# A test of the softmax sums at the end of the kernel, and a second path behind a branch

## The chip, the cores and the metric

The kernel runs on one core of a Trainium2 chip. The metric is the device time of one execution in microseconds. The engines of a core are TensorE (PE, matmuls), VectorE (DVE), ScalarE (ACT), GpSimd (POOL) and SyncE (SP). Each has its own queue of instructions and runs it in order; between queues, semaphores say what is done. PEld is PE's loading of weights, and a name with a q (ACTq) is an engine's queue itself, for example when it issues a transfer.

## The reference

The first half is a dynamic convolution: each position has its own softmax weights over its last 7 positions, for each of 8 heads of 24 columns. The second half is a layer with two input matrices, an elementwise maximum and an output matrix.

```
x: (8, 4160, 192) = 0.1 * normal;  weight_gen: (8, 4160, 8 heads, 7 taps) = 0.3 * normal
w = exp(weight_gen - max over taps);  w = w / (sum of w over taps + 1e-9)
y[s] = sum over taps t of w[s, head, t] * x[s - 6 + t]      (zeros ahead of each sequence)
h1 = y @ w1;  h2 = y @ w2                                   (192 -> 1024)
out = maximum(h1, h2) @ w_out                               (1024 -> 192), 33280 rows
```

## The kernel before

The 33,280 rows lie over 128 partitions, 260 neighbouring rows ("columns" in the code, `CPP`) on each. The columns go in 17 batches of 16 (the last has 4). The softmax is computed without the maximum: `exp_sum(b)` takes the exponential of a batch on ScalarE, `red(b)` sums the 7 taps on VectorE (L147), `ln(b)` takes the logarithm of the sum in place on ScalarE (L151), `shift(b)` subtracts it from the raw weights on VectorE (L156), and `weights(b, o)` takes the exponential again on ScalarE, now normalized, in bfloat16 (L167). The sums of a batch live in a tile from a pool with three buffers, `psm`, so they are gone three batches later.

`mul` and `adds` (L182, L198, L202, L205) form and add the seven products on VectorE; a DMA transposes the result (L214), and GpSimd's small `gate` cast (L222) waits for that transposition before GpSimd issues the next loads. On PE, `hid_tile` (L297) makes the hidden layer as differences of the two matrices, `relu` (L307, ScalarE) moves it out of PSUM, and the output comes from two kinds of matmuls, `out_first` (L349 with the product of w1 and w_out, and half of L337) and `out_second` (the other half of L337). Because max(h1, h2) = h1 + relu(h2 - h1), this gives the reference's maximum. `evac` copies results out of PSUM on ScalarE (L393) and has SyncE store them.

The order of each queue is written out by hand (a manual schedule): what stands earlier in the code is earlier in its engine's queue. The end is `rest_of_results` (L484): the last columns in three parts, `out_first` of each ahead of `out_second` of the one before, and `evac` behind it. The last `evac` copies into `o_last` (L381), and ScalarE and SyncE issue one store each (L384). Behind that stands the closing block (line L801 in the profile): SyncE waits for all transfers and engines, every queue drains, and GpSimd gathers and releases all five queues, twice.

Of the kernel before, what the change touches and what calls it, by code (L numbers as in the profile page):

```python
# [9 lines left out]
FP32 = mybir.dt.float32  # L10
BF16 = mybir.dt.bfloat16
I32 = mybir.dt.int32
AF = mybir.ActivationFunctionType
ALU = mybir.AluOpType
AX = mybir.AxisListType


def _sub(base: bass.AP, off: int, dims):
    ap = [list(base.ap[0])] + [[int(s), int(c)] for s, c in dims]
    return dataclasses.replace(base, offset=base.offset + off, ap=ap)  # L20
# [3 lines left out]
def kernel(  # L24
# [9 lines left out]
    nc = tc.nc  # L34

    B, S, D = x.shape
    H, K = weight_gen.shape[2], weight_gen.shape[3]
    F = moe_w1.shape[1]
    P = 128
    PAD = K - 1  # L40
    WGC = H * K
    FCH = F // P
    HF = F // 2
    CPP = B * S // P
    RPB = P // B
    G = D // H
# [3 lines left out]
    BATCHES = [(c, min(16, CPP - c)) for c in range(0, CPP, 16)]  # L50
    NB = len(BATCHES)
# [11 lines left out]
    UNITS = []  # L63
    for b, (c0, n) in enumerate(BATCHES):
# [3 lines left out]
    TILES = [(u, k) for u, (_, _, n) in enumerate(UNITS) for k in range(n)]  # L68
# [6 lines left out]
    consts = ctx.enter_context(tc.tile_pool(name="consts", bufs=1))  # L75
    pwg = ctx.enter_context(tc.tile_pool(name="pwg", bufs=4))
    pxb = ctx.enter_context(tc.tile_pool(name="pxb", bufs=2))
    pe_ = ctx.enter_context(tc.tile_pool(name="pe", bufs=2))
    psm = ctx.enter_context(tc.tile_pool(name="psm", bufs=3))
    pm = ctx.enter_context(tc.tile_pool(name="pm", bufs=1))  # L80
    pen = ctx.enter_context(tc.tile_pool(name="pen", bufs=2))
    py = ctx.enter_context(tc.tile_pool(name="py", bufs=2))
    pyt = ctx.enter_context(tc.tile_pool(name="pyt", bufs=6))
    prd = ctx.enter_context(tc.tile_pool(name="prd", bufs=7))
    first_ps = ctx.enter_context(ExitStack())
    ps = {k: first_ps.enter_context(tc.tile_pool(name="pps_" + k, bufs=2, space=bass.MemoryType.PSUM))
          for k in ("h", "o")}
# [6 lines left out]

    wg_ts, xb_ts, e_ts, s_ts, en_ts, y_ts, yt_ts = {}, {}, {}, {}, {}, {}, {}

    m_t = pm.tile([P, K * 16 * D], BF16, name="m_t")
# [37 lines left out]
    def part(b, i, of):  # L137

        n = BATCHES[b][1]
        h0, h1 = n * i // of * H, n * (i + 1) // of * H  # L140
        return slice(h0, h1), h0 * K, [[K, h1 - h0], [1, K]]

    def red(b, i=0, of=1):
        if i == 0:
            s_ts[b] = psm.tile([P, BATCHES[b][1] * H], FP32, name="sum_t", tag="sum")
        hs, at, ap = part(b, i, of)
        nc.vector.reduce_sum(out=s_ts[b][:, hs], in_=_sub(e_ts[b], at, ap), axis=AX.X)  # L147

    def ln(b, i=0, of=1):
        s_t = s_ts[b][:, part(b, i, of)[0]]  # L150
        ln_of[b] = nc.scalar.activation(out=s_t, in_=s_t, func=AF.Ln)  # L151

    def shift(b, i=0, of=1):
        hs, at, ap = part(b, i, of)
        w_t = _sub(wg_ts[b], at, ap)
        nc.vector.tensor_tensor(out=w_t, in0=w_t, in1=_sub(s_ts[b], hs.start, [[1, hs.stop - hs.start], [0, K]]),  # L156
                                op=ALU.subtract)

    def weights(b, o):
# [73 lines left out]
    def half(j):  # L233
        return slice(64 * j, 64 * j + 64)
# [23 lines left out]
    relu_of, yt_of, w10_of, ln_of = {}, {}, [], {}  # L258
# [6 lines left out]
    rd_at, hd_at, op_at, o_t = {}, {}, {}, []  # L265
# [43 lines left out]

    def column(c):  # L310

        b = min(c // 16, NB - 1)
        for u, (ub, o, n) in enumerate(UNITS):
            if ub == b and o <= c - BATCHES[b][0] < o + n:
                k = c - BATCHES[b][0] - o
                return u, k // 2, k % 2

    def place(p):
# [5 lines left out]
    def op_out(c):  # L324

        tile_, at = op_at[c // 2]
        return tile_[:, at + c % 2 * 512:at + c % 2 * 512 + D]

    def out_hidden(c, f, r):

        u, i, j = column(c)
        t0 = TILES.index((u, 0))
        if UNITS[u][2] == 8:
            (rd, k), at = rd_at[t0 + f], j * 512 + i * P
        else:
            (rd, k), at = rd_at[t0 + f // 2], j * 512 + f % 2 * 256 + i * P
        return nc.tensor.matmul(  # L337
            op_out(c), lhsT=rd[half(r), k * 1024 + at:k * 1024 + at + P],
            rhs=wo[half(r), f * D:(f + 1) * D], start=False, stop=(r != j and f == FCH - 1),
            skip_group_check=True,  # L340
        )

    def out_first(now):

        for c in now[::2]:
            u, i, _ = column(c)
            for s in range(3):
                for j in range(2):
                    nc.tensor.matmul(  # L349
                        op_out(c + j),  # L350
                        lhsT=yt_ts[u][half(j), (3 * i + (s + j) % 3) * P:(3 * i + (s + j) % 3 + 1) * P],
                        rhs=w10[half(j), s * D:(s + 1) * D], start=(c == now[0] and s == 0),
                        stop=False, skip_group_check=True,
                    )
            for f in range(FCH):
                last = [out_hidden(c + j, f, j) for j in range(2)]
        return last

    def out_second(now, go):

        for c in now[::2]:
            for f in range(FCH):
                for j in range(2):
                    mm = out_hidden(c + 1 - j, f, j)
                    if c == now[0] and f == 0:
                        tc.add_manual_dep(mm.ins, go.ins.name, SYNC, reason="bank of the other half")

    def relay(last):

        go = nc.scalar.nop()  # L370
        for mm in last:
            tc.add_manual_dep(go.ins, mm.ins.name, SYNC, reason="bank of the other half")
        return go
# [52 lines left out]
    OUTS, c = [[], [], []], 0  # L426
    for g in range(3, len(GROUPS)):
        most = 4 if g == 3 else 2 if GROUPS[g][1] == 2 or len(OUTS[-1]) == 4 else 4
        n = min(most, ready[g] - c)
# [5 lines left out]
    def room(g):  # L435

        t0, n = GROUPS[g]
        if "c" in ps:
            for t, k in zip(range(t0, t0 + n), "abc"[:n - 1] + "c"):
                hd_at[t] = ps[k].tile([P, 1024], FP32, name="hd" + k, tag=k), 0  # L440
        else:
            for t in range(t0, t0 + n):
                hd_at[t] = ps["h"].tile([P, 1024], FP32, name="hdp", tag="hd"), 0
        rd = prd.tile([P, 3 * 1024], BF16, name="rd_t", tag="rd")
        for t in range(t0, t0 + n):
            rd_at[t] = (rd, t - t0)
        return rd

    def out_room(now, tag=None):
        tag = tag or ("r" if "r" in ps else "o")  # L450
        tile_ = ps[tag].tile([P, 1024], FP32, name="op_ps", tag=tag if tag in "abc" else "op")
        for c in now:
            op_at[c // 2] = tile_, (c - now[0]) // 2 * D

    def hidden(g, now=(), between=lambda: None, beside=lambda: None, ahead=lambda: None,
# [25 lines left out]
        if len(now) <= 2:  # L481
            beside()

    def rest_of_results(c):  # L484

        parts = [p for p in (c[:4], c[4:-2], c[-2:]) if p]
        assert max(map(len, parts)) <= 4
        go = []
        for i, now in enumerate(parts):
            out_room(now, ("r", "a", "c")[i])  # L490
            go.append(relay(out_first(now)))
            if i:
                out_second(parts[i - 1], go[i - 1])
                evac(parts[i - 1][0] // 2, len(parts[i - 1]) // 2)
        out_second(parts[-1], go[-1])
        evac(parts[-1][0] // 2, len(parts[-1]) // 2)
# [6 lines left out]
    ident = consts.tile([P, P], BF16, name="ident")  # L503
    msk_i = consts.tile([P, 1], I32, name="msk_i")
    msk = consts.tile([P, 1], FP32, name="msk")
    gate = consts.tile([P, 1], FP32, name="gate")
    o_last = consts.tile([P, 2 * D], FP32, name="o_last")

    with tc.tile_pool(name="pstage", bufs=1) as pstage:
# [7 lines left out]
        for p0, p1 in ((1, 16), (16, P)):  # L517
            nc.sync.dma_start(
                out=xs[p0:p1, 0:PAD * D],
                in_=bass.AP(tensor=x.tensor, offset=(p0 * CPP - PAD) * D,  # L520
                            ap=[[CPP * D, p1 - p0], [1, PAD * D]]),
# [20 lines left out]
        for wi, wsrc in enumerate((moe_w1, moe_w2)):  # L542
            for h in range(2):
                nc.sync.dma_start(  # L544
                    out=ws["T", wi][half(h), :],
                    in_=bass.AP(tensor=wsrc.tensor, offset=P * F + h * HF, ap=[[F, 64], [1, HF]]),
# [11 lines left out]
        for step in (exp_sum, red, ln, shift):  # L558
            for i in range(2):
# [4 lines left out]
                                op0=ALU.mult)  # L564
        nc.scalar.activation(out=xb_ts[0][:, HP:PAD * D], in_=xs[:, HP:PAD * D], func=AF.Copy,
                             scale=msk[:, 0:1])
        for o in (0, 4, 8, 12):
            weights(0, o)
        nc.vector.tensor_copy(out=xb_ts[0][:, PAD * D:(PAD + 4) * D],
                              in_=xs[:, PAD * D:(PAD + 4) * D])  # L570
# [36 lines left out]
        def keep_warm(times):  # L607
# [11 lines left out]
            out=wo[:, :].rearrange("p (f d) -> p f d", d=D),  # L619
            in_=bass.AP(tensor=moe_w_out.tensor, offset=0, ap=[[D, P], [P * D, FCH], [1, D]]),  # L620
# [9 lines left out]
        rd = room(0)  # L630
# [43 lines left out]
        rd = room(3)  # L674
# [17 lines left out]
        rd = room(4)  # L692
# [2 lines left out]

    pout = ctx.enter_context(tc.tile_pool(name="pout", bufs=1))
    o_t.append(pout.tile([P, 24 * D], FP32, name="o_t", tag="o"))


    def rest_of_1():  # L700
# [64 lines left out]
    for g in range(4, len(GROUPS)):  # L765
# [7 lines left out]
        else:  # L773
            hidden(g, OUTS[g], beside=lambda: steps(g, tiles), before=lambda: softmax_steps(g, 0),
                   after=lambda: softmax_steps(g, 1))
    rest_of_results(OUTS[-1])

# [1 line left out]
_INS = ['x', 'weight_gen', 'moe_w1', 'moe_w2', 'moe_w_out']  # L779
# [26 lines left out]
```

## Time and profile before

| what | value |
|---|---|
| median of 3 timed runs | 408.99 us (406.66 to 411.06) |
| the profiled execution | 406.16 us |
| its span, first to last instruction | 404.3 us |
| outside the span | 1.9 us |
| busy in the span: PE, DVE, ACT, POOL | 98%, 92%, 89%, 19% |
| granted TensorE clock, mean | 0.999 |

A timeline row has the start in the span, the length, the engine, the source line, the operation, what it writes and reads, and how many such instructions it joins. A group's row ends with total busy time and the mean of one in nanoseconds, and then idle time ahead of it with what ended that. In the records of one source line, the three numbers behind an operation are its shortest, median and longest duration in nanoseconds, and then come the first and the last start in microseconds. The digits are the busy tenths of 40 equal slices of 10.1 us. In the list of DMA queues a row has packets, megabytes and the share of the time of 16 DMA engines.

### The profile page before, as it was taken

Reading aid. Unit: us, or ns where it says so; the run is one execution under the profiler, and the core shown is the slowest. Engines: PE = TensorE matmul, PEld = TensorE weight load, DVE = VectorE, ACT = ScalarE, POOL = GpSimd, SP = SyncE. Lnnn points to the kernel's source line nnn. Section 1 sums busy time; section 2 is a strip of 40 time slices with the busy share of each in tenths; the row PEclk is TensorE's granted clock in tenths of the full one; section 3 lists DMA queues with packets and bytes.
Section 4 is the critical chain, followed back from the end, with each engine's and each line's share of the span. In section 5 each row is a group of like instructions: output and inputs, shape, how many; then the busy total and the mean of one; then the engine's idle time right before and its main releaser. Section 6 shows DMA issues by size and latency. Waiting matters only on the chain.

```text
span 404.3 us, 16242 instructions
## 1 busy us (share of the span) xinstructions
PE 397.3 (98%) x7458; PEld 318.6 (79%) x7458; DVE 370.3 (92%) x215; ACT 360.7 (89%) x462; POOL 76.3 (19%) x101
## 2 busy tenths in 40 slices
PE   7999999999999999999999999999999999999996
PEld 2699999777777787778777778877787877777795
DVE  5999999999999999999999999999999999999100
ACT  6899999999999989999899999989999899897872
POOL 0311130212222011222221212222012222110000
PEclk9999999999999999999999999999999999999999
DMA  8956549876757855774775587577548647743614
GB/s 250 232 120 184 157 98 245 149 174 155 194 90 232 191 111 121 229 204 78 233 201 109 115 237 203 74 236 200 110 111 240 170 70 241 154 89 51 246 41 158
DMA packets 60785, 65.70 MB, mean 163 GB/s; under 512 B 47631, under 2 KB 49039, under 8 KB 60718
## 3 DMA queue, kind: packets, MB, share of 16 engines
q1 hardware_dynamic: 52334, 40.54, 35.6%
q0 software_dynamic: 8240, 24.04, 29.2%
q8 instruction: 58, 0.95, 0.9%
q10 hardware_dynamic: 144, 0.10, 0.1%
q14 instruction: 9, 0.07, 0.1%
HBM read 35.96 MB, written 25.56 MB: 152 GB/s over the span
## 4 chain that ended last, share of the span: by engine, by line
PE 92%; ACT 3%; DMA 2%; SPq 1%; issue 0%; DVE 0%; DVEq 0%; ACTq 0%
PE op_ps L337 42%; PE hdc L297 13%; PE hda L297 13%; PE hdb L297 13%; PE op_ps L349 8%; PE yps L246 2%; DMA ws1T<-in_moe_w_dram 2%; ACT rd_t L307 1%; PE hdp L297 1%; SPq L544 0%; ACT yt L253 0%; PE pw L652 0%; ACT w1t L670 0%; ACT e_t L135 0%; SPq L536 0%
## 5 line engine op out<-in xcount | busy, mean ns | idle before, releaser
L337 PE MATMUL op_ps<-wo,rd_t 64*128 64x192 bf16 x4160 | 210.3, 243 | 0.0
L337 PEld LDWEIGHTS <-rd_t 64*128 64x128 bf16 x4160 | 180.6, 94 | 15.5
L182 DVE TENSOR_TENSOR m_t<-xb_t,en_t 128x10752 bf16<-128x10752 bf16 (+1 forms) x37 | 187.4, 5070 | 0.3
L297 PEld LDWEIGHTS <-wd 64*128 64x128 bf16 x1776 | 93.4, 94 | 40.1 <-issue 1.1
L307 ACT ACTIVATE rd_t<-hdc 128x1024 bf16<-128x1024 f32 x82 | 84.0, 1024 | 17.6 <-PE hdc L297 15.9
L222 POOL CAST gate<-yt 128x1 f32<-128x1 bf16 x29 | 41.1, 1416 | 267.3 <-DMA yt<-y_t 267.3
L307 ACT ACTIVATE rd_t<-hdb 128x1024 bf16<-128x1024 f32 x81 | 83.6, 1032 | 0.0
L307 ACT ACTIVATE rd_t<-hda 128x1024 bf16<-128x1024 f32 x81 | 83.4, 1030 | 0.0
L198 DVE TENSOR_TENSOR m_t<-m_t 128x4608 bf16<-128x4608 bf16 (+1 forms) x29 | 72.7, 2508 | 0.1
L297 PE MATMUL hdc<-yt,wd 64*128 64x512 bf16 (+1 forms) x534 | 67.8, 359 | 0.0
L393 ACT COPY o_t<-op_ps 128x384 f32<-128x384 f32 (+1 forms) x99 | 56.3, 579 | 12.6 <-PE op_ps L337 12.6
L297 PE MATMUL hda<-yt,wd 64*128 64x512 bf16 (+1 forms) x528 | 67.0, 359 | 0.0
L297 PE MATMUL hdb<-yt,wd 64*128 64x512 bf16 (+1 forms) x522 | 67.0, 362 | 0.0
L349 PE MATMUL op_ps<-w,yt 64*128 64x192 bf16 x780 | 55.3, 243 | 0.0
L349 PEld LDWEIGHTS <-yt 64*128 64x128 bf16 x780 | 38.8, 94 | 15.6 <-issue 0.5
L202 DVE TENSOR_TENSOR m_t<-m_t 128x3072 bf16<-128x3072 bf16 (+1 forms) x29 | 49.9, 1722 | 0.1
L167 ACT ACTIVATE en_t<-wg_t 128x896 bf16<-128x896 f32 (+2 forms) x45 | 35.2, 809 | 2.0 <-PE op_ps L337 2.0
L205 DVE TENSOR_TENSOR y_t<-m_t 128x1536 bf16<-128x1536 bf16 (+1 forms) x29 | 27.3, 941 | 0.5
L114 POOL DMA_DIRECT2D xb_t<-in_x_dram x33 | 18.0, 546 | 21.3 <-DVE m_t L182 10.4
L156 DVE TENSOR_TENSOR wg_t<-wg_t,sum_t 128x280 f32<-128x280 f32 (+5 forms) x46 | 22.0, 481 | 0.0
L147 DVE TENSOR_REDUCE sum_t<-e_t 128x64 f32<-128x448 f32 (+2 forms) x31 | 19.5, 633 | 2.3 <-ACT e_t L135 2.3
L135 ACT ACTIVATE e_t<-wg_t 128x896 f32<-128x896 f32 (+2 forms) x18 | 15.9, 889 | 2.3 <-DMA wg_t<-in_weight_gen_dram 2.3
(49 smaller groups left out, 117.1 us busy)
## 6 DMA issues: line engine op xcount, KB each, us to landing
out_dram<-o_t SPq DMA_DIRECT2D x27, 768.0 KB, 4.5
xb_t<-in_x_dram POOLq DMA_DIRECT2D x30, 384.0 KB, 4.9
wg_t<-in_weight_gen_dram POOLq DMA_DIRECT2D x14, 448.0 KB, 5.6
xb_t<-xb_t POOLq DMA_DIRECT2D x16, 288.0 KB, 5.1
out_dram<-o_t SPq DMA_DIRECT2D x10, 384.0 KB, 3.1
wg_t<-in_weight_gen_dram SPq DMA_DIRECT2D x2, 448.0 KB, 4.2
xs<-in_x_dram SPq DMA_DIRECT2D x2, 384.0 KB, 6.0
xb_t<-in_x_dram POOLq DMA_DIRECT2D x3, 192.0 KB, 4.6
```

Of the source, the lines that this page charges most:

```text
L156: nc.vector.tensor_tensor(out=w_t, in0=w_t, in1=_sub(s_ts[b], hs.start, [[1, hs.stop - hs.start], [0, K]]), op=ALU.subtract)
L167: nc.scalar.activation(out=_sub(en_ts[b], (o * WGC + j * N * K) * 2, [[2 * N, K], [2, N], [1, 2]]), in_=_sub(wg_ts[b], (o * H + j * N) * K ...
L182: return nc.vector.tensor_tensor(out=m_out, in0=x_in, in1=_sub(en_ts[b], o * WGC * 2, [[2, K * n * H], [0, G // 2], [1, 2]]), op=ALU.mult,)
L198: nc.vector.tensor_tensor(out=taps(0, 1, 3), in0=taps(0, 1, 3), in1=taps(3, 1, 3), op=ALU.add)
L202: nc.vector.tensor_tensor(out=taps(0, 2, 2), in0=taps(0, 2, 2), in1=taps(1, 5, 2), op=ALU.add)
L205: nc.vector.tensor_tensor(out=_sub(y_ts[b], o * D, [[64, 2], [P, 3 * w // 2], [1, 64]]), in0=taps(0, 1, 1), in1=taps(2, 1, 1), op=ALU.add,)
L222: nc.gpsimd.tensor_copy(out=gate, in_=yt[:, 0:1])
L297: nc.tensor.matmul(hid_out(t, f, j), lhsT=wd_at(j, s, f // 4, f % 4 * P, P), rhs=_sub(yt_ts[u][half(j), :], (s + j) % 3 * P, [[3 * P, w // ...
L307: relu_of[t0] = nc.scalar.activation(out=rd[:, k * 1024:(k + n) * 1024], in_=hd[:, at:at + n * 1024], func=AF.Relu)
L337: return nc.tensor.matmul(op_out(c), lhsT=rd[half(r), k * 1024 + at:k * 1024 + at + P], rhs=wo[half(r), f * D:(f + 1) * D], start=False, s ...
L349: nc.tensor.matmul(op_out(c + j), lhsT=yt_ts[u][half(j), (3 * i + (s + j) % 3) * P:(3 * i + (s + j) % 3 + 1) * P], rhs=w10[half(j), s * D: ...
L393: nc.scalar.copy(out=_sub(o, c % 24 * D, [[D, len(qs)], [h * D, 2], [1, D]]), in_=_sub(tile_, at + (qs[0] - p) * D, [[D, len(qs)], [512, 2 ...
```

## The change

The sums of all batches are kept: `red` writes into slices of two tiles that live to the end, `sums` (128 columns) and `sums_later` (the other 132), and `ln` writes its logarithm to a tile of its own, which `shift` reads. In `rest_of_results`, after the first part's `out_first`, a test follows: the largest and the smallest sum of each partition are compared with 1e15 and 1e-15, and a matmul with one column on each side counts the partitions that are good. At the very end four engines (all but SyncE) load that count into a register and branch: where it is not 128, a second path computes all 260 columns again, four at a time and with the maximum subtracted first, written out without a loop, with its transfers on GpSimd.

```
 def red(b, i=0, of=1):
     if i == 0:
-        s_ts[b] = psm.tile([P, BATCHES[b][1] * H], FP32, name="sum_t", tag="sum")
+        c0, n = BATCHES[b]
+        at = c0 - 128 if c0 >= 128 else c0
+        s_ts[b] = sums[c0 >= 128][:, at * H:(at + n) * H]
+        ln_ts[b] = psm.tile([P, n * H], FP32, name="ln_t", tag="ln")
...
 def ln(b, i=0, of=1):
-    s_t = s_ts[b][:, part(b, i, of)[0]]
-    ln_of[b] = nc.scalar.activation(out=s_t, in_=s_t, func=AF.Ln)
+    hs = part(b, i, of)[0]
+    ln_of[b] = nc.scalar.activation(out=ln_ts[b][:, hs], in_=s_ts[b][:, hs], func=AF.Ln)
...
+LOW, HIGH = 1e-15, 1e15
+def test_sums():
+    good, ones = in_range[:, 4:5], in_range[:, 5:6]
+    for i, s in enumerate(sums):
+        nc.vector.tensor_reduce(out=in_range[:, i:i + 1], in_=s, axis=AX.X, op=ALU.max)
+        nc.vector.tensor_reduce(out=in_range[:, 2 + i:3 + i], in_=s, axis=AX.X, op=ALU.min)
+    nc.vector.memset(ones, 1.0)
+    nc.vector.tensor_scalar(out=in_range[:, 0:2], in0=in_range[:, 0:2], scalar1=HIGH, scalar2=None, op0=ALU.is_le)
+    nc.vector.tensor_scalar(out=in_range[:, 2:4], in0=in_range[:, 2:4], scalar1=LOW, scalar2=None, op0=ALU.is_ge)
+    nc.vector.tensor_reduce(out=good, in_=in_range[:, 0:4], axis=AX.X, op=ALU.min)
+    found = ps["b"].tile([P, 1024], FP32, name="found", tag="b")
+    nc.tensor.matmul(found[0:1, 0:1], lhsT=good, rhs=ones, start=True, stop=True)
+    nc.vector.tensor_copy(out=count, in_=found[0:1, 0:1])
...
 def rest_of_results(c):
...
         go.append(relay(out_first(now)))
+        if i == 0:
+            test_sums()
...
+sums = [consts.tile([P, 128 * H], FP32, name="sums")]
+in_range = consts.tile([P, 6], FP32, name="in_range")
+count = consts.tile([1, 1], I32, name="count")
...
+sums.append(pout.tile([P, (CPP - 128) * H], FP32, name="sums_later"))
...
 rest_of_results(OUTS[-1])
+ET = mybir.EngineType
+good = nc.values_load(count, engines=[ET.PE, ET.Activation, ET.DVE, ET.Pool], min_val=0, max_val=P,
+                      skip_runtime_bounds_check_because="a count of partitions")
+with tc.If(good != P, preferred_fallthrough_block=False):
+    with_maximum()
```

`with_maximum()` calls `columns(c)` 65 times, for c = 0, 4, ... 256. Each loads the raw weights and the rows, subtracts the maximum, takes the exponential, the sum and the logarithm, multiplies, adds the taps by matmuls as `sum_transpose` does, and runs hidden layer and output as the main path does:

```
+        def columns(c):
+            nc.gpsimd.dma_start(out=wt[:, 0:WB], in_=...)
...
+            softmax_of(ALU.max, wt)
+            less()
+            nc.scalar.activation(out=et[:, 0:WB], in_=wt[:, 0:WB], func=AF.Exp)
+            softmax_of(ALU.add, et)
...
+        for c in range(0, CPP, 4):
+            columns(c)
```

In the built program, the second path stands between the short block that the branch falls into when all is good and the closing block. It has 27,042 instructions for PE, 1,166 for ScalarE, 463 for VectorE and 346 for GpSimd, and none for SyncE.

More of the change, by code (lines that the diff above doesn't have):

```diff
@@ L93, in later_ps @@
             ps[k] = ctx.enter_context(tc.tile_pool(name="pps_" + k, bufs=1, space=bass.MemoryType.PSUM))
+    ln_ts = {}
     wg_ts, xb_ts, e_ts, s_ts, en_ts, y_ts, yt_ts = {}, {}, {}, {}, {}, {}, {}
@@ L155, in shift @@
         w_t = _sub(wg_ts[b], at, ap)
-        nc.vector.tensor_tensor(out=w_t, in0=w_t, in1=_sub(s_ts[b], hs.start, [[1, hs.stop - hs.start], [0, K]]),
+        nc.vector.tensor_tensor(out=w_t, in0=w_t, in1=_sub(ln_ts[b], hs.start, [[1, hs.stop - hs.start], [0, K]]),
                                 op=ALU.subtract)
@@ L310, in column @@
     def column(c):
[L312 to L315, printed above, removed]
+        for u, (b, o, n) in enumerate(UNITS):
+            k = c - BATCHES[b][0] - o
+            if 0 <= k < n:
                 return u, k // 2, k % 2
@@ new lines, in with_maximum, with softmax_of, less @@
+    def with_maximum():
+        u, T = len(UNITS), len(TILES)
+        BATCHES.append((CPP, 4))
+        UNITS.append((NB, 0, 4))
+        TILES.extend((u, k) for k in range(4))
+        WB = 4 * WGC
+        xt = pxb.tile([P, (16 + PAD) * D], BF16, name="xb_t", tag="xb")
+        wt = pwg.tile([P, 16 * WGC], FP32, name="wg_t", tag="wg")
+        et = pe_.tile([P, 16 * WGC], FP32, name="e_t", tag="e")
+        en = pen.tile([P, 16 * WGC * 2], BF16, name="en_t", tag="en")
+        st = psm.tile([P, 16 * H], FP32, name="ln_t", tag="ln")
+        yt = pyt.tile([P, 8 // 2 * 3 * P], BF16, name="yt", tag="yt")
+        rds = [prd.tile([P, 3 * 1024], BF16, name="rd_t", tag="rd") for _ in range(2)]
+        yps = ps["r"].tile([P, 1024], FP32, name="yps", tag="op")
+        o = o_t[0]
+        def softmax_of(op, tile_):
+            nc.vector.tensor_reduce(out=st[:, 0:4 * H], in_=_sub(tile_, 0, [[K, 4 * H], [1, K]]), axis=AX.X, op=op)
+        def less():
+            nc.vector.tensor_tensor(out=wt[:, 0:WB], in0=wt[:, 0:WB], in1=_sub(st, 0, [[1, 4 * H], [0, K]]),
+                                    op=ALU.subtract)
+        def columns(c):
+            nc.gpsimd.dma_start(out=wt[:, 0:WB], in_=bass.AP(
+                tensor=weight_gen.tensor, offset=c * WGC, ap=[[CPP * WGC, P], [1, WB]]))
+            before = min(c, PAD)
+            if before < PAD:
+                h = (PAD - before) * D
+                nc.vector.memset(xt[:, 0:h], 0.0)
+                for p in range(0, P, RPB):
+                    nc.gpsimd.dma_start(out=xt[p + 1:p + RPB, 0:h], in_=bass.AP(
+                        tensor=x.tensor, offset=((p + 1) * CPP + c - PAD) * D, ap=[[CPP * D, RPB - 1], [1, h]]))
+            nc.gpsimd.dma_start(out=xt[:, (PAD - before) * D:(PAD + 4) * D], in_=bass.AP(
+                tensor=x.tensor, offset=(c - before) * D, ap=[[CPP * D, P], [1, (before + 4) * D]]))
+            softmax_of(ALU.max, wt)
+            less()
+            nc.scalar.activation(out=et[:, 0:WB], in_=wt[:, 0:WB], func=AF.Exp)
+            softmax_of(ALU.add, et)
+            nc.scalar.activation(out=st[:, 0:4 * H], in_=st[:, 0:4 * H], func=AF.Ln)
+            less()
+            N = 2 * H
+            for j in range(2):
+                nc.scalar.activation(out=_sub(en, j * N * K * 2, [[2 * N, K], [2, N], [1, 2]]),
+                                     in_=_sub(wt, j * 2 * WGC, [[1, K], [K, N], [0, 2]]), func=AF.Exp)
+            nc.vector.tensor_tensor(
+                out=_sub(m_t, 0, [[64, 2], [P, K * 6], [1, 64]]),
+                in0=_sub(xt, 0, [[2 * D, 2], [D, K], [1, 2 * D]]),
+                in1=_sub(en, 0, [[2, K * 4 * H], [0, G // 2], [1, 2]]), op=ALU.mult,
+            )
+            for k in range(6):
+                for t in range(K):
+                    at = (t * 6 + k) * P
+                    for r in range(2):
+                        nc.tensor.matmul(
+                            yps[:, r * 512 + k * 64:r * 512 + (k + 1) * 64],
+                            lhsT=m_t[half(r), at:at + P], rhs=ident[half(r), half(r)],
+                            start=(k == 0 and t == 0), stop=(t == K - 1), skip_group_check=True,
+                        )
+            nc.scalar.copy(out=_sub(yt, 0, [[64, 2], [P, 6], [1, 64]]), in_=_sub(yps, 0, [[512, 2], [64, 6], [1, 64]]))
+            yt_ts[u] = yt
+            for t in range(T, T + 4):
+                tag = "abc"[(t - T) % 3]
+                hd_at[t] = ps[tag].tile([P, 1024], FP32, name="hd" + tag, tag=tag), 0
+                rd_at[t] = rds[(t - T) // 2], (t - T) % 2
+                hid_tile(t)
+                relu(rd_at[t][0], t, 1)
+            now = list(range(CPP, CPP + 4))
+            out_room(now, "a")
+            out_second(now, relay(out_first(now)))
+            tile_, at = op_at[CPP // 2]
+            nc.scalar.copy(out=_sub(o, 0, [[D, 2], [2 * D, 2], [1, D]]),
+                           in_=_sub(tile_, at, [[D, 2], [512, 2], [1, D]]))
+            nc.gpsimd.dma_start(out=bass.AP(tensor=out.tensor, offset=c * D, ap=[[CPP * D, P], [1, 4 * D]]),
+                              in_=o[:, 0:4 * D])
+        for c in range(0, CPP, 4):
+            columns(c)
```

## The prediction

> **What bounds the kernel now.** I read the page's first, second and fourth parts, then the timeline of the last ten microseconds, then the queue records of the closing line L801, because all that the change executes stands at the end.
>
> ```profile
> span 404.3 us, 16242 instructions
> PE 397.3 (98%) x7458; PEld 318.6 (79%) x7458; DVE 370.3 (92%) x215; ACT 360.7 (89%) x462; POOL 76.3 (19%) x101
> ...
> DVE  5999999999999999999999999999999999999100
> ...
> PEclk9999999999999999999999999999999999999999
> ...
> q8 instruction: 58, 0.95, 0.9%
> ...
> q14 instruction: 9, 0.07, 0.1%
> ...
> PE 92%; ACT 3%; DMA 2%; SPq 1%; issue 0%; DVE 0%; DVEq 0%; ACTq 0%
> ```
>
> The chain that ended last is TensorE for 92% of the span at the full granted clock, so time added to PE's order of matmuls counts in full. VectorE is nearly as busy (92%), but its digits fall to 1, 0, 0: it has nothing to do in the last 29 us. That is the cover of the test.
>
> The timeline from there to the end:
>
> ```profile
> 374.75 0.56 DVE L205 TENSOR_TENSOR y_t<-m_t 128x768 bf16<-128x768 bf16 x1
> ...
> 395.82 0.41 PE L349 MATMUL op_ps<-w,yt 64*128 64x192 bf16 x6
> 396.06 2.14 PE L337 MATMUL op_ps<-wo,rd_t 64*128 64x192 bf16 x48
> ...
> 400.48 0.48 ACT L381 COPY o_last<-op_ps 128x384 f32<-128x384 f32 x1
> 400.98 0.34 SPq L384 DMA_DIRECT2D out_dram<-o_last  x1
> 400.99 0.38 ACTq L384 DMA_DIRECT2D out_dram<-o_last  x1
> ```
>
> After the last matmul come a copy on ScalarE, two transfers (SyncE and ScalarE issue one each), and the wait for them. ScalarE's queue has issued its own at 401.37. What the queues do from then on is in the records of L801, and the last transfer's flight is in the answer for its tile:
>
> ```profile
> L801 SPq DRAIN  x3: 7/7/13, 403.4 to 403.7; - x3
> L801 POOLq DRAIN  x3: 46/98/5591, 379.6 to 404.0; - x3
> L801 PEldq DRAIN  x2: 13/556/1098, 399.4 to 403.8; - x2
> L801 ACTq DRAIN  x2: 8/78/148, 401.4 to 403.8; - x2
> ...
> DMA to landing us min/median/max: 1.8/1.9/2.0
> ```
>
> SyncE waits for the landings until 403.45 and then drains; GpSimd gathers the five queues; 0.8 us later the span ends. The others stand at the barrier early: ScalarE from 401.5, PE from 400.5, GpSimd from 385.2 (its first drain took 5.59 us). So ScalarE has **1.9 us of slack**, and no more.
>
> **The change part by part.** *Sums kept, logarithm in its own tile.* In the built program the order and the waits of all five queues are the same as before up to the test, so the main part neither gains nor loses an instruction: Ln reads and writes as many elements, 0.33 us as on L151 before. Addresses in SBUF move; no row prices that, and I take 0.
>
> *Test on VectorE.* Two reductions over 128x1024 and two over 128x1056. The nearest rows:
>
> ```profile
> L147 DVE TENSOR_REDUCE sum_t<-e_t 128x64 f32<-128x448 f32 x26 | 15.8, 610 | 2.3 <-ACT e_t L135 2.3
> L147 DVE TENSOR_REDUCE sum_t<-e_t 128x128 f32<-128x896 f32 x3 | 3.2, 1083 | 0.0
> ```
>
> 448 elements more cost 473 ns, so 1.06 ns each: 1.22 us for 1024 and 1.25 us for 1056, 4.9 us for the four. Memset, two comparisons and a reduction over 4 are small (the 128x1 TENSOR_SCALAR of L555 took 154 ns): 0.6 us. It runs from 375.3 to 380.8. Its reader is the new 1x1 matmul, which stands behind the first `out_first` of `rest_of_results`, at 396.0. Cost 0, covered by 15 us of matmuls; without the cover 5.5 us would stand on PE's path.
>
> *The 1x1 matmul `found`.* It is on PE's path. Matmuls here follow each other every 41 ns (16 of L337 in 0.66 us in the chain); that is the lower bound. The upper one is a full-array weight load and matmul that overlap nothing: 0.15 us (L610) and 0.22 us (L598). No fp32 matmul is in the trace. I take **0.2 us**, bounds 0.04 to 0.4. It moves all that follows on PE, and so the last copy and the last issues.
>
> *Copy of `count`, four loads into registers, four compare-and-branch.* VectorE, GpSimd, PE and ScalarE each load `count` and branch; SyncE does not. The path not taken by the data is laid out between: each of the four falls into a short block (semaphores set to what the second path would have left) and jumps from there over the second path to the barrier. What is behind the load on each queue is only that and the barrier.
>
> No load into a register is in the trace. Below stands a semaphore instruction (17 ns), above the shortest transfer (1.8 us). Nearest in kind is work that a sequencer does itself, the 0.38 us of ScalarE's DMA issue: I take 0.4 us. A branch: between 0.02 us (semaphore) and 0.15 us (ACT's drain); I take 0.05.
>
> The jump is the dear part. The page's q8 row moves 0.95 MB in 58 packets, 16 KB each, and PE's 14,918 instructions make 0.95 MB at 64 bytes: instructions come in by DMA as the queue goes on, up to the end. One such packet takes 0.9% of 16 x 404.3 us, divided by 58: 1.0 us; on q14 (0.1%, 9 packets) 0.7 us. The second path has 1,166 instructions for ScalarE (75 KB), 27,042 for PE (1.7 MB). q14 brought 0.07 MB in the whole run, so what lies 75 KB ahead is not likely to be there. Lower bound 0 (it is at hand); middle 2.5 us, the shortest flight of 1.8 us and one packet of 0.7 us; upper 7.6 us, by the longest flight of the run, 6.9 us in the crowded first stage (ws0T), and the packet. I take 2.5 us, since at the end the DMA engines are nearly empty, as for the last transfer's 1.8 to 2.0 us.
>
> [...]
>
> ScalarE: 401.37 + 0.2 (found) + 0.4 (load) + 0.05 + 0.03 (two semaphores) + 0.05 + 2.5 (jump) + 0.15 (drain) = 404.75, against the 403.45 of SyncE. The barrier's 0.8 us follow: 405.55, so **+1.3 us** with `found` in it. PE gets to its load at 399.6 and to the barrier at about 403.0 (0.55 us, then 1.8 + 1.0): hidden. VectorE and GpSimd branch when `count` is there, near 396.6, and would be through the jump at 399.7: hidden.
>
> The profiled execution took 406.16 us, 1.9 us outside its span; with 1.3 us it is 407.5. The median of the runs shown, 408.99, is 2.8 us above the profiled one, and its runs scatter by 2.2 us. Against it the forecast is 410.3 us.
>
> **Rivals.**
>
> *Hidden.* The jump's target is at hand or arrives in under 1.2 us (the time that would still end before SyncE's 403.65). For it: in the run before, ScalarE's branch into the closing block cost under 0.05 us (issue ends 401.37, drain at 401.4). Against it: that block lay next in the program. Only `found` is left, +0.2 us: 409.2 us.
>
> *GpSimd last.* Its first drain of 5.59 us moves behind the branch. Drain from 399.7 to 405.3, then 0.8 us: +1.8 us, 410.8 us. For it: the drain was that long with no transfer of its own in flight for 25 us (last issue 353.5). Against it: it followed directly on the last `gate` cast, and if it waited for that cast alone it is short at 399.7 (its later ones took 46 and 98 ns).
>
> *Slower: a long jump on ScalarE.* At the upper bound, 7.6 us, ScalarE stands at the barrier at 409.85, the span ends at 410.65, +6.35 us: 415.3 us. It decides alone from a jump of 5.3 us on (1% is 4.09 us). For it: landings of 4.5 to 6.9 us are usual in the page's issues, and more than one piece may be wanted. Against it: the engines are empty then, and the last landings took 1.8 to 2.0 us.
>
> *The second path runs.* The reference draws the weights as 0.3 times a normal number; seven exponentials sum to about 7, far from 1e-15 and 1e15. If it ran, its 13,520 matmuls alone would add 554 us at 41 ns: about 960 us. The program allows it, these data don't.
>
> **How the numbers follow.** Forecast (ScalarE's jump last, 1 to 3 us) 0.41; hidden 0.17; GpSimd last 0.14; long jump 0.22; second path 0.01; scatter of the runs that shows as faster 0.05. The runs shown scatter by 1% (406.66 to 411.06), so 1% is about what a measurement of this kernel can tell from no change. Within 1% are the first three: 0.72. Slower: 0.22 + 0.01. Faster: 0.05, since nothing is taken out. Range: from the hidden case less the scatter and a little (409.2 - 2.4 = 406.8) to the long jump (415.3).
>
> **What would show it.** Right: four reductions on VectorE of 1.2 us each from 375.3; PE without a pause around `found`; VectorE's records ending near 381 but for the 1x1 copy near 396.5; ScalarE's first drain in the closing block at 404 to 405, later than SyncE's landings; the last-barrier stretch of 0.8 us unchanged; a few more instruction packets than 58. Wrong: ScalarE's drain before 403.5 (hidden), GpSimd's first drain ending last, a pause on PE at 396 (the test is not covered), or main-part instructions with other durations (addresses matter).

## The result, and the profile after

| | before | changed |
|---|---|---|
| median of 19 timed runs | 408.03 us (405.8 to 412.69) | 411.93 us (409.76 to 415.06) |
| the profiled execution | 406.16 us | 412.54 us |
| its span | 404.3 us | 410.7 us |

The ratio of the changed kernel to the one before is 1.0091, 95% interval 1.0067 to 1.0116: slower by 3.7 us, within the 1% of the forecast, though nearly three times the 1.3 us in its sum.

The two spans differ by 6.4 us, and only a part of that is the change. I split each span at the start of the `o_last` copy and call the rest the **tail**. The copy starts at 400.48 us before and 403.40 us after; the tail is 3.81 us before and 7.27 us after. The 2.9 us ahead of the copy arise early, 2.4 us of them by 28 us and 2.8 by 51 us, in and just behind the stage where the weights come in (ws1T flew 6.5 us before and 7.7 us here); from there the distance between the two kernels stays at 2.7 to 2.8 us until `found` adds its 0.2. They are scatter: in the fourteen profiles of this study the copy starts anywhere between 400.5 and 404.6 us, at 401.21 in a second profile of the changed kernel, and at 403.24 in one of a kernel with neither test nor branch. So the profiles are compared by their tails, and the test by its own rows.

The timeline of the changed kernel around the test (start, length, engine, line, operation):

```profile
377.65 1.21 DVE L493 TENSOR_REDUCE in_range<-sums 128x1 f32<-128x1024 f32 x1
...
381.06 1.25 DVE L494 TENSOR_REDUCE in_range<-sums_later 128x1 f32<-128x1056 f32 x1
...
398.83 0.15 DVE L501 CAST count<-found 1x1 int32<-1x1 f32 x1 [16.13 <-PE found L500]
...
403.40 0.48 ACT L384 COPY o_last<-op_ps 128x384 f32<-128x384 f32 x1
403.91 0.38 ACTq L387 DMA_DIRECT2D out_dram<-o_last  x1
```

The reductions are where they were put (later by the shift of the main part) and as long as forecast, and the result waits 16 us for TensorE. In the chain that ended last, the piece of `found` and the last copy, and behind them the piece of the kernel before that follows the same matmuls:

```profile
398.68 0.12 PE found L500 x2
...
403.40 0.48 ACT o_last L384
```

```profile
395.98 0.25 PE op_ps L349 x6
```

From the end of the first part's matmuls to the copy it is 4.72 us here (398.68 to 403.40) and was 4.50 us before (395.98 to 400.48): `found` costs 0.22 us. The rest is in the tail. The records of the load (L887), of the branch (L889) and of the closing block (L915), one fence each, and the last stores' flight from the answer for `o_last`:

```profile
L887 POOLq TENSOR_LOAD <-count x1: 721/721/721, 399.0 to 399.0; - x1
...
L887 ACTq TENSOR_LOAD <-count x1: 563/563/563, 404.3 to 404.3; - x1
```

```profile
L889 PEldq COMPARE_BRANCH  x2: 90/1876/3663, 402.9 to 403.6; - x2
L889 ACTq COMPARE_BRANCH  x2: 38/46/53, 405.0 to 405.2; - x2
...
L889 POOLq INC_SWDGE_SEM  x1: 1487/1487/1487, 400.2 to 400.2; - x1
```

```profile
L915 POOLq DRAIN  x3: 46/106/5445, 404.4 to 410.4; - x3
L915 SPq DRAIN  x3: 7/7/13, 407.7 to 410.1; - x3
...
L915 PEldq DRAIN  x2: 8/38/68, 407.3 to 410.2; - x2
L915 ACTq DRAIN  x2: 8/44/80, 407.8 to 410.1; - x2
```

```profile
DMA to landing us min/median/max: 3.2/3.3/3.4
```

GpSimd loads at 399.0, spends 1.49 us on a semaphore update in the short block, jumps at 401.7, drains at 404.4 for 5.45 us and so reaches the barrier at 409.83. ScalarE (407.87), SyncE (407.82) and TensorE (407.34) have stood there for two microseconds or more. The jump itself shows as the gap between the last branch and the drain (ScalarE 405.24 to 407.79, 2.55 us), or, on TensorE, as the length of the branch (3.66 us). What the prediction did not have is the last line: the last stores, the same bytes from the same copy, take 3.3 us instead of 1.9.

```profile
q8 instruction: 60, 0.98, 1.0%
q14 instruction: 15, 0.12, 0.1%
```

That is 2 and 6 packets of instructions more than before, and they come at the end: from 400 us on, 3 on q8 and 6 on q14, against one on q8 and none on q14 from 397 us on before. I take the packets of q8, 16 KB each, for TensorE's and those of q14, 8 KB each, for the other engines': among the last stores there is one of 16 KB where TensorE alone jumps far (one step, below), and there are only 8 KB ones where it does not jump.

### The profile page after: what moved, and what is told of

Read it like the earlier page. It is cut to its first block, busy times and chain, and to the rows that moved or that the text cites. A ratio compares the mean times of both kernels' runs of the same rounds, so it can differ in the third digit from the quotient of the medians.

```text
span 410.7 us, 16278 instructions
## 1 busy us (share of the span) xinstructions
PE 397.7 (97%) x7460; PEld 319.0 (78%) x7460; DVE 375.8 (91%) x224; ACT 361.0 (88%) x462; POOL 75.2 (18%) x101
## 4 chain that ended last, share of the span: by engine, by line
PE 92%; DMA 2%; DVE 2%; issue 1%; SPq 1%; ACT 0%; DVEq 0%
PE op_ps L340 42%; PE hdc L301 13%; PE hda L301 13%; PE hdb L301 13%; PE op_ps L352 8%; PE yps L250 2%; DMA ws1T<-in_moe_w_dram 2%; PE hdp L301 2%; DVE m_t L186 1%; SPq L652 1%; PE pw L760 0%; DVE sums L151 0%; SPq L644 0%; SPq L626 0%; DVE wd L687 0%
## 5 line engine op out<-in xcount | busy, mean ns | idle before, releaser
L226 POOL CAST gate<-yt 128x1 f32<-128x1 bf16 x29 | 40.0, 1381 | 267.9 <-DMA yt<-y_t 267.9
L160 DVE TENSOR_TENSOR wg_t<-wg_t,ln_t 128x280 f32<-128x280 f32 (+5 forms) x46 | 22.0, 481 | 0.0
L311 ACT ACTIVATE rd_t<-hdp 128x1024 bf16<-128x1024 f32 x16 | 15.9, 1046 | 0.0
```

The costliest lines, as they stand in the source:

```text
L160: nc.vector.tensor_tensor(out=w_t, in0=w_t, in1=_sub(ln_ts[b], hs.start, [[1, hs.stop - hs.start], [0, K]]), op=ALU.subtract)
L226: nc.gpsimd.tensor_copy(out=gate, in_=yt[:, 0:1])
L311: relu_of[t0] = nc.scalar.activation(out=rd[:, k * 1024:(k + n) * 1024], in_=hd[:, at:at + n * 1024], func=AF.Relu)
```

## The experiments

Each experiment is an edit of the kernel before or of the changed kernel; the later ones add to the early drain step by step. Tails and flights are from one profiled execution each; ratios, with 95% intervals, compare the timed runs to the kernel before on the same chip.

| kernel | tail, us | flight of the last stores, median us | ratio to before |
|---|---|---|---|
| before | 3.81 | 1.9 | |
| changed | 7.27 | 3.3 | 1.0091 (1.0067 to 1.0116) |
| changed, again | 7.31 | 3.6 | 1.0084 (1.0047 to 1.0121) |
| before, with a GpSimd cast at the end | 7.01 | 1.9 | 1.0105 (1.0029 to 1.0181) |
| changed, early drain | 5.77 | 3.8 | 1.0045 (1.0006 to 1.0084) |
| changed, test only | 3.83 | 1.9 | 1.0017 (0.9983 to 1.0051) |
| changed, second path of one step | 5.43 | 3.5 | 1.0094 (1.0054 to 1.0133) |
| early drain, no TensorE in the second path | 5.25 | 2.7 | 1.0041 (1.0000 to 1.0082) |
| early drain, early loads | 5.90 | 4.0 | 1.0048 (1.0014 to 1.0082) |
| the same, jump at the branch | 5.40 | 3.5 | 1.0025 (0.9991 to 1.0059) |
| the same, with a hint | 5.57 | 3.7 | 1.0073 (1.0045 to 1.0100) |
| hint, no early drain | 5.39 | 3.5 | 1.0018 (0.9990 to 1.0046) |
| early drain, hint, later jump on TensorE | 3.90 | 2.0 | 0.9978 (0.9945 to 1.0011) |
| changed, transfers by ScalarE, branch on SyncE | 6.81 | 3.9 | 1.0113 (1.0051 to 1.0176) |

**GpSimd's drain alone, in the kernel before.**

```
             nc.scalar.copy(out=_sub(o_last, ...), in_=_sub(tile_, at, ...))
+            nc.gpsimd.tensor_copy(out=gate, in_=o_last[:, 0:1])
```

> Kernel before, with one more GpSimd cast (128x1) that reads o_last and so stands after the last copy on ScalarE. 'Tail' is the time from the start of the o_last copy to the end of the span: 3.8 us before, 7.3 us after the change. Theory 'GpSimd drain': GpSimd's first drain in the closing block costs about 5.5 us wherever it stands. The cast ends about 0.8 us after the copy's start, the drain at 6.3, the barrier adds 0.8: tail 7.1 us, about 3.3 us slower than before, with no branch in the kernel. Rival 'jump': the drain was long before only because of what GpSimd had just done at 380 us; here it is under 0.2 us, tail 3.8 us, no difference.

```profile
L802 POOLq DRAIN  x3: 46/107/5592, 403.8 to 410.0; - x3
L802 SPq DRAIN  x3: 7/7/13, 406.2 to 409.7; - x3
```

Tail 7.01 us, 3.2 us more than before, without a branch in the kernel. SyncE is ready at 406.2 and waits for GpSimd until 409.4. The drain theory holds: the 5.59 us stood in the kernel before all along, under TensorE's last 21 us of matmuls.

**The drain put early, in the changed kernel.**

```
         nc.vector.tensor_copy(out=count, in_=found[0:1, 0:1])
+        nc.gpsimd.drain()
```

> Changed kernel, with a drain of GpSimd put ahead of its register load, where it has nothing to do. Theory 'GpSimd drain': that drain takes 5.5 us from about 382 us on, under TensorE's work; the one in the closing block is then under 0.2 us, the barrier waits for ScalarE's jump and SyncE's landings instead (407.9 in the changed kernel's trace), tail 5.3 us, 2.0 us faster than the changed kernel and 1.6 us slower than before. Rival: the long drain comes from the semaphore update or the jump ahead of it; it is 5.4 us again, tail 7.3 us, no gain.

```profile
L502 POOLq DRAIN  x1: 5592/5592/5592, 379.7 to 379.7; - x1
```

```profile
L890 POOLq INC_SWDGE_SEM  x1: 171/171/171, 397.5 to 397.5; - x1
```

```profile
L916 POOLq DRAIN  x3: 34/106/118, 400.7 to 406.2; - x3
L916 SPq DRAIN  x3: 7/7/13, 405.6 to 405.9; - x3
```

The drain moves under the matmuls at its full length, the one in the closing block takes 0.12 us, and the semaphore update falls from 1.49 to 0.17 us. Tail 5.77 us, 1.5 us less. I had expected 5.3: SyncE now comes last, because the stores flew 3.8 us.

**The test alone.** The loads, the branch and the second path are left out.

> Changed kernel without the register loads, the branch and the second path: the sums kept and the test up to the copy of the count remain. All theories: the test is covered and only the 1x1 matmul shows, 0.2 us between the neighbouring matmuls; tail 3.8 us, the last stores land in 1.8 to 2.0 us, time within 0.3 us of before. Rival 'moved addresses': main-part instructions got slower, and 1 us or more of the 3.7 us stays.

Tail 3.83 us, flight 1.9 us, ratio 1.0017 with 1 inside its interval. Addresses and test cost nothing that this measurement can tell (its interval still allows 2 us); by the tails, all that the change adds behind the copy comes with the branch.

**A short second path.** Only the first of the 65 steps is left (`range(0, 4, 4)`).

> Changed kernel with the second path cut to its first step (4 of 260 columns), so that the closing block lies 14 instructions further on ScalarE, 418 on TensorE (26 KB), 14 on GpSimd and 11 on VectorE, instead of 1166, 27042, 346 and 463. Theory 'fetch': no queue stalls at its jump (under 0.3 us from the last branch to the drain, 2.6 to 3.7 us in the changed kernel), and the last stores land in about 1.9 us again instead of 3.3. GpSimd gets to its drain 2.6 us earlier and keeps the 5.4 us: the drain ends 3.9 us after the start of the o_last copy, tail 4.7 us, 1.1 us slower than before. Rival 'branch': the jump costs the same at any distance; tail 7.3 us.

```profile
L889 PEldq COMPARE_BRANCH  x2: 90/1976/3863, 400.7 to 401.3; - x2
L889 ACTq COMPARE_BRANCH  x2: 38/46/53, 402.7 to 402.9; - x2
```

```profile
L915 POOLq DRAIN  x3: 46/102/5372, 399.6 to 406.3; - x3
...
L915 ACTq DRAIN  x2: 8/8/8, 403.1 to 406.1; - x2
L915 PEldq DRAIN  x2: 8/38/68, 405.2 to 406.1; - x2
```

Over 14 instructions ScalarE's jump takes 0.1 us (branch at 402.95, drain at 403.1) and over 1,166 it took 2.55, so it is not the branch itself that costs. I put the difference down to bringing the instructions in: in the changed kernel two packets of q14 (405.45 and 406.11 us) start within ScalarE's 2.55 us. But TensorE stalls 3.86 us over 418 instructions too, and the stores still fly 3.5 us. I had expected both to go, and GpSimd's drain, which ended at 405.0, to come last instead of SyncE (405.8). The stores gave the next clue: in the trace's landing records each store has 16 parts, and 15 of them land within 2.5 us of the copy's start, as before, while one lands 1.6 to 1.8 us later. TensorE's packet of 16 KB starts 1.39 us after the copy's start and takes 1.2 us.

The ratio of this kernel, 1.0094, does not show the 1.8 us that its tail is shorter than that of the changed kernel. Some 0.8 us of it lies outside the span: that part is 2.5 to 2.7 us in each of its runs, and 1.7 to 2.2 us in all runs of the other edits. Why, no run shows; the rest is as much as the main part scatters.

**Who holds the stores up.** The early drain, and no work for TensorE in the second path.

> Changed kernel with the early GpSimd drain, and the second path without TensorE: its matmuls are left out and its copies read SBUF, so TensorE has no load and no branch, while ScalarE, VectorE and GpSimd jump as far as before (780, 462 and 346 instructions). Theory 'TensorE's fetch is what holds the last stores up': ScalarE still stalls about 2.6 us at its jump and stands at the barrier 4.4 us after the start of the o_last copy, but the last stores land in at most 2.2 us (3.8 with the early drain alone, 3.5 in the one-step kernel, whose only far jump was TensorE's); tail 5.2 us. Rival 'any fetch': ScalarE's fetch holds them up as much, landing 3.3 us or more, tail 5.6 us or more.

Flight 2.7 us, between the two theories: 14 of 16 parts of each store on time, the other two up to 0.8 us late. The 8 KB packets of q14 take 0.3 us (three of them, 0.8 to 2.9 us behind the copy; the trace does not tell whose each is). So I take both kinds of packet to hold stores up, TensorE's twice as much (a part 1.6 to 1.8 us late in the one-step kernel, up to 0.8 us here). The number of late parts goes with the number of packets: one packet and one late part of each store in the one-step kernel, here two packets within 1 us of the copy's start and two late parts. ScalarE, at its drain 4.38 us after the copy's start, now comes last; tail 5.25 us as expected.

**Loads ahead, and the jump ahead.** First the registers are loaded in `rest_of_results`, behind the middle part; then the second path is laid out directly behind the branch as well.

```
+            if i == 1:
+                found_good.append(nc.values_load(count, engines=[...], ...))
...
-    with tc.If(good != P, preferred_fallthrough_block=False):
+    with tc.If(found_good[0] != P, preferred_fallthrough_block=True):
```

> Changed kernel with the early GpSimd drain and the registers loaded behind the middle part of the last results, the layout unchanged. Theory: TensorE's jump stands behind a semaphore that waits for its last matmul and starts no earlier, so its stall and the late landing stay; only ScalarE arrives 0.5 us earlier. Tail 5.2 to 5.8 us, within 0.4 us of the early drain alone. Rival 'the loads are what is dear': 0.5 us and more faster than the early drain alone.

> Changed kernel with the early GpSimd drain, the registers loaded behind the middle part of the last results, and the second path laid out directly behind the compare-and-branch, so that the jump over it is the compare-and-branch itself, ahead of the semaphore that waits for the last matmul. Theory: TensorE jumps about 1.0 us before its last matmul ends instead of 0.2 us behind it, its packet of instructions is through before most of the last stores' packets, and it stands at the barrier 2.8 us after the start of the o_last copy instead of 4.4; ScalarE jumps 0.8 us earlier, at the barrier at 3.5; last stores land in 2 to 3 us. Tail 4.3 to 4.8 us, 1 us faster than with the early drain alone and 0.7 us slower than before. Rival: the fetches meet the stores just the same, tail 5.5 us.

The loads alone gave nothing (5.90 us against 5.77). With the jump at the branch TensorE jumps 1.1 us before the copy and stands at the barrier at 3.4, but its packet starts only 1.9 us after the jump, 0.85 us behind the copy's start, again among the stores: 3.5 us of flight, tail 5.40 us. Three packets (one of TensorE, two of 8 KB) start 0.85 to 0.95 us behind the copy's start, and three parts of each store are late. Rival confirmed; the theory of the earlier jump falls.

**The target named ahead.** A hint for the branch (BRANCH_PREFETCH_HINT in the records, at 0.7 to 0.8 us) is put at the start of the main part, on the four engines.

```
+    tc.mark_branch_hint_location("all_good", engines=[ET.PE, ET.Activation, ET.DVE, ET.Pool])
```

> The kernel with the jump at the branch (early GpSimd drain, early loads, second path directly behind the compare-and-branch), and an instruction at the start of the main part on the four branching engines that names the coming branch's target for the instruction prefetch. Theory 'fetch': with the target's instructions brought in ahead, no queue stalls at its compare-and-branch (under 0.2 us, TensorE 4.3 us without the hint), no packet of instructions falls among the last stores, they land in 1.9 us, SyncE's landings end last as before; tail 3.8 to 4.0 us, time within 0.4 us of before, 1.4 us faster than without the hint. Rival 'the branch, not the fetch': stalls and late landings stay, tail 5.4 us.

> The same without the early GpSimd drain: GpSimd does its long semaphore update (1.5 us) and the 5.4 us drain behind the branch. Theory: without its stall at the jump GpSimd starts its drain about 2.0 us before the o_last copy and ends it 3.5 us after, together with SyncE's landings; tail 3.9 to 4.4 us. Rival: the drain counts in full, tail 7 us as in the changed kernel.

TensorE's branch without the hint (L894) and with it (L896):

```profile
L894 PEldq COMPARE_BRANCH  x1: 4293/4293/4293, 401.7 to 401.7; - x1
```

```profile
L896 PEldq COMPARE_BRANCH  x1: 1022/1022/1022, 402.4 to 402.4; - x1
```

The stalls shrink: TensorE's branch takes 1.02 us instead of 4.29, and it drains 0.15 us behind the copy's start. The late landing stays (3.7 and 3.5 us): TensorE still has a packet of 16 KB at 1.3 to 1.5 us after the copy's start, and one part in 16 of each store is late again. What is in that packet, the trace does not say. Without the early drain GpSimd, no longer stalled at the jump, ends its 5.4 us at 4.1 us, ahead of SyncE at 4.6: tail 5.39 us. The ratios of these two lie further apart than their tails (1.0073 and 1.0018); I have no cause for that.

**The jump moved behind the stores.** TensorE waits for the `o_last` copy before it branches.

```
+            tc.add_manual_dep(nc.tensor.nop().ins, copied.ins.name, SYNC, reason="jump behind the last stores")
```

> The kernel with the hint and the early GpSimd drain, and on TensorE a wait for the o_last copy ahead of its compare-and-branch, so that it jumps 0.6 us behind the copy's start instead of 1.1 us ahead of it. Theory: with the hint TensorE still starts a fetch of the block behind its target 2.4 us after the jump (1.4 us behind the copy's start), and that packet of 1 us is what holds one part in 16 of each last store up; 1.7 us later it meets no store any more. Landing 1.9 to 2.2 us, TensorE at the barrier at 1.8, SyncE as before; tail 3.8 to 4.2 us, time within 0.4 us of before and 3 us faster than the changed kernel. Rival: the late part has another cause, or ScalarE's packet at 2.0 us takes its place: landing 3 us or more, tail 5 us or more.

```profile
L897 PEldq COMPARE_BRANCH  x1: 483/483/483, 405.1 to 405.1; - x1
L897 ACTq COMPARE_BRANCH  x1: 68/68/68, 405.5 to 405.5; - x1
```

```profile
L923 POOLq DRAIN  x3: 34/51/97, 402.1 to 408.2; - x3
L923 SPq DRAIN  x3: 7/7/13, 407.7 to 408.0; - x3
```

```profile
DMA to landing us min/median/max: 1.8/2.0/2.1
```

Tail 3.90 us, flight 2.0 us: SyncE comes last, as in the kernel before, and the whole second path stands behind the branch. TensorE's packet now starts 2.27 us behind the copy's start, when the parts are all but through (the last lands at 2.6), and no part is late. The collision of TensorE's packet with the stores is thereby shown, by moving it in time alone. Against the kernel before the ratio is 0.9978 (0.9945 to 1.0011), no difference that this measurement can tell; both intervals of the changed kernel lie wholly above it.

**GpSimd without a branch.** The second path's transfers are issued by ScalarE, with rows loaded as fp32 and converted by a copy, and SyncE branches.

> Changed kernel with the second path's transfers issued by ScalarE instead of GpSimd (the rows loaded as fp32 and converted by a copy); SyncE then loads and branches instead of GpSimd, over one instruction. Theory: GpSimd reaches its drain at about 380 us and is out of the way as in the kernel before; the end is set by ScalarE's and TensorE's jumps and the stores that land late, as with the early drain; SyncE's own load (0.5 us) lies beside the stores. Tail 5.5 to 6.0 us, 1.5 us faster than the changed kernel. Rival: SyncE's branch takes GpSimd's place (it has to wait for the landings, then set semaphores, then jump), tail 7 us or more.

Tail 6.81 us, between theory and rival and nearer to the rival. GpSimd drains at 379.8 and is out of the way, but SyncE sits at its short block until the late stores have landed, branches 4.99 us after the copy's start and then works through the closing block's own semaphores, 0.9 us more. Ratio 1.0113: no gain over GpSimd.

> The changed kernel as it is, beside the others on the same chip. Theory: GpSimd's drain of 5.4 us ends last again, tail 7.3 us, the last stores land in over 3 us, 0.7 to 1.2% slower than before.

The changed kernel once more: tail 7.31 us, GpSimd's drain of 5.45 us last, 1.0084. The tail repeats to 0.05 us.

## Why the prediction was right or wrong

**Right.** The main part is untouched; the four reductions took 1.21 to 1.25 us (1.22 and 1.25 forecast) and are covered; `found` cost 0.22 us (0.2); the second path did not run. ScalarE's jump stalled 2.55 us (2.5) over 1,166 instructions, and 0.1 us over 14 in the one-step kernel. The others stalled 2.9 us on VectorE, 2.6 on GpSimd and 3.7 to 4.3 on TensorE. That in this time the instructions come in by DMA is my reading, from the packets that start within these stalls of the changed kernel (one of q8 in TensorE's, two of q14 in each of the others'). The register loads, 0.4 us in the sum, took 0.49 to 0.72 us.

**Wrong: who comes last.** The forecast was ScalarE; it was the rival "GpSimd last", given 0.14. What I held against it, that the drain might only wait for the `gate` cast, is refuted by the late cast and the early drain: the first drain after GpSimd's transfers took 5.4 to 5.6 us wherever these runs put it (from 379.6 us on before, 403.8 behind the late cast, 404.4 in the changed kernel), and the next ones 0.03 to 0.12. What it does in that time, no run here shows. (The 25 us in the argument for that rival count from the last issue; the transfer landed at 357.4 us, 22 us ahead of the drain.)

**Wrong in size: the terms of that rival.** It was priced at +1.8 us and the tail gained 3.46. The step that failed is GpSimd's way from `count` to its drain: 3.1 us in the prediction (396.6 to 399.7), 5.4 measured (398.98 to 404.38). In it the load took 0.72 us instead of 0.4, and the short block, for which only a few hundredths were allowed, 0.5 us up to its last wait and 1.49 us for a semaphore update. Jump (2.6 for 2.5) and drain (5.45 for 5.59) were right. The update is short (0.17 us) where a drain has stood ahead, which suggests that both wait for the same unfinished work.

**Wrong: two steps called hidden.** TensorE's jump starts behind a semaphore that waits for its last matmul, which I had not counted, and it stalls 3.7 to 4.3 us; at 3.9 us behind the copy it is still not what ends last. But the instruction packets (one of q8 1.34 us behind the copy's start, three of q14 at 0.94 to 2.71) held up parts of the last stores, which flew 3.3 us instead of 1.9, and so SyncE is ready at 407.8 instead of 406.4. This is why the early drain gained 1.5 us and not the 2.0 I expected. I took the landings of the end as given; the change reached them through its instruction packets.

**The sum as it is.** `found` 0.22 us; tail 3.46 us. Of it the early drain takes off 1.50 (7.27 to 5.77), which is what GpSimd's drain and update cost beyond the rest; the other 1.96 (5.77 to 3.81) is SyncE's wait for the late stores (they flew 3.8 us there; with the hint and TensorE's packet moved behind them 2.0, and the tail was 3.90). Together 3.7 us, or 0.9% of 408, as measured. That the time came out within the forecast 1% is in part luck: the engine that comes last was another, the sum was 2.4 us short, and 0.4 us more would have left the 1%.

## What to carry to other kernels

Work that no engine's busy time shows can stand at the end of a queue, hidden only by its early place, as GpSimd's drain of 5.59 us from 379.6 us on did here: before anything is put behind it, look in the records of the closing block at how long each queue's first drain takes, and drain early where it is free (1.5 us of tail here). The branch over the long path cost ScalarE little as an instruction here (0.04 to 0.05 us); the jump over 1,166 instructions cost it 2.55 us (0.1 over 14), and the last stores flew 3.3 us instead of 1.9 beside the instruction packets. Naming its target early cut TensorE's branch from 4.29 to 1.02 us, and placing the jump behind the last stores as well brought the tail to 3.90 us. At an end of 4 us, count each queue from the last matmul on; the main part's scatter of 4 us hides it.

## What the runs showed of the hardware

GpSimd's first drain took 5.4 to 5.6 us, 26 to 48 us after its last transfer was issued, and its semaphore update 1.49 us, or 0.17 us behind a drain. Instruction packets held up the last stores: with one 16 KB packet of 0.9 to 1.2 us among them, one part in 16 of each store landed 1.5 to 1.8 us late; with that packet 2.27 us behind the copy's start, none did. TensorE stalled 3.86 us at a jump over 418 instructions, where ScalarE took 0.1 us over 14. With a hint given 400 us ahead TensorE's branch took 0.48 to 1.02 us instead of 4.29.
